# Second copies of a weight matrix made by ScalarE, VectorE and GpSimd in place of transfers, first weight passes spread over three engines, and new places for the opening's work

## The chip, the cores and the metric

The kernel runs on one core of a Trainium2 chip. The metric is the device time of one execution in microseconds: the median of 3 timed runs, 860.36 us before the change (859.08 to 860.88). Five engines work side by side, each in the order of its own instruction stream, and wait for one another through semaphores: TensorE (PE, its weight loads shown as PEld), VectorE (DVE), ScalarE (ACT), GpSimd (POOL) and SyncE (SP), which here only issues transfers. The transfers are carried by 16 DMA engines.

## The reference, cut to what matters

```python
# attention: q, k, v (8 batches, 8 heads, 576 tokens, 64 wide), tau = 0.02, float32
scores = (q @ k.T) / 8
thresh = scores.max(-1) - tau
scores = where(scores >= thresh, scores, -1e9)
attn = softmax(scores);  x = attn @ v          # heads side by side: (4608, 512)
# feed-forward: w_in (512, 1024), w_out (1024, 512), g_ln (1024)
h = x @ w_in
solu = h * softmax(h)
ln = (solu - mean(solu)) / sqrt(var(solu) + 1e-6) * g_ln
out = ln @ w_out                               # (4608, 512) float32
```

w_in and w_out arrive as 64-bit floats (a float32 array times a NumPy scalar), so that the kernel itself makes 32-bit floats of their words.

## The kernel before, in words

**Rounds.** The attention is cut into 144 slots (`slots`, L447): batch, kind (first or second 256 queries of a head pair, or the last 64 of all pairs), head pair, half. One round of the loop at L1426 handles one slot. Its phases, in order: `begin` jobs; `scores` (PE, L478); `maxes` (DVE, L500), `ramp` (ACT, L515), `exps` (ACT, L524); `early` jobs; `normalise` of the slot before (POOL, L531 to L534); `middle` jobs; matmuls of attention times v (`attend_steps`, L605, called pv below) and of the feed-forward; `blocks` of the slot before (DVE transposes, L545), and after every second slot `spread` (SP, L566 to L575), which moves the transposed weights T to wT; `late` jobs; loads. A pv comes `LAG_PV` = 3 rounds after its second slot, plus `LAG`. After it ACT copies the result (`attended`, L638).

**Opening and steady part.** Rounds 0 to 29 are the opening, rounds from START = 30 on the steady part, with other tables and PSUM tiles. In the opening the weights are decoded, the keys and queries of batches 0 and 1 are turned on PE (`turn`, L346) and kept in SBUF by ACT and DVE (`k_item`, `q_item`, `e_item`; with `EASED` the second half goes to ACT too, without it to DVE), and four tiles of 128 tokens of the feed-forward, the fronts (L1284), are run: two h steps each, a chain of jobs, two o steps, at the rounds in `HO`. `PREP` says in which round's score tile each turning is placed, `FETCH` at which round's end each load of batches 0 and 1 is issued. Up to START, `CHAIN` gives each job of a front (max, exp, mul, sum, stats, norm, norm2, turn, out, store) a phase (0 begin to 3 late) and a number of rounds after the front's second h step.

**Weights.** There are 16 pieces of 128 rows: 0 to 7 are halves of w_in, 8 to 15 are blocks of w_out. Each goes through

- `weight_load` (L261): a transfer of 512 KB to one of four raw buffers (`RAW`), which is free again after `weight_a`;
- `weight_a` (L273): three passes over the raw words: z, the high words times 2**-112 (L282 to L286, on the engine that `UNIT` names: 0 DVE, 1 ACT, 2 POOL), sg, the sign bits (L291, DVE), and the low words times 2**-29 into the destination (L294, ACT);
- `weight_b` (L306, DVE): z shifted, sg put in; `weight_c` (L316, POOL): added to the destination;
- `weight_gain` (pieces 8 to 15, L318): times g_ln, on the engine in `GAIN` (0 ACT, 1 DVE, 2 POOL);
- `weight_d` (pieces 8 to 15, L329): the second copy. PE works on 64 x 64 quarters, and `ff_o` (L1128) needs each block of w_out in both halves of the rows. So rows 0 to 63 are copied to rows 64 to 127 of the neighbouring slot of w2 and the reverse, 128 KB each, by two transfers on SP.

`PIECE` holds five places for each piece (load, a, b, c, gain and copy), counted in quarters of a round: 4 x round + phase. `weigh` (L1298) is called four times a round (before the scores, before `normalise`, after it, and at the end) and issues what is due. At a round's end everything but gain and copy stands ahead of the round's other loads, gain and copy behind them. The first o step of front 0 is in round 17, its second in round 18; the first uses pieces 8 to 11, the second 12 to 15.

**Feed-forward.** `ff_h` L1021, `ff_max`, `ff_exp` L1045, `ff_mul` L1051, `ff_sum`, `ff_stats` L1067, `ff_scale` (POOL, L1075 to L1082), `ff_norm` (ACT, L1094), `ff_norm2` (L1099: DVE, or POOL where `SECOND` says so), `ff_swap` (four transfers, L1112), `ff_turn` (DVE, L1123), `ff_o` L1141, `ff_out`, `ff_store`.

All transfers of the opening but the first few are issued by SP in program order; one that waits holds back all behind it.

Of the kernel before, what the change touches and what calls it, by code (L numbers as in the profile page):

```python
# [13 lines left out]
ALU = mybir.AluOpType  # L14
# [6 lines left out]
def kernel(  # L21
# [27 lines left out]
    nc = tc.nc  # L49
# [279 lines left out]
    def weight_d(x):  # L329
        c = x - 2 * NP  # L330
        if c >= 0:
            for r in range(2):
                nc.sync.dma_start(out=w2[ROWS[r], 2 * c + 1], in_=w2[ROWS[1 - r], 2 * c])
# [929 lines left out]
    with tc.manual_schedule():  # L1263
# [283 lines left out]
```

## Time and profile before

| | us |
|---|---|
| median of 3 runs (lowest, highest) | 860.36 (859.08, 860.88) |
| the profiled execution's own time | 858.72 |
| its span, first to last instruction | 856.9 |
| PE busy | 805.5 (94%) |
| DVE busy | 674.0 (79%) |
| ACT busy | 598.7 (70%) |
| POOL busy | 553.8 (65%) |
| start of round 0, 9, 11, 17, 19, 30 (first L500 of each) | 10.90, 53.69, 68.63, 102.96, 117.87, 172.78 |
| L333 (second copies): 16 issues, first and last | 61.8, 108.7 |
| first part of a wT spread, issue to landing, up to 130 us: least, median, greatest | 5.4, 8.0, 10.7 |

The page's line of busy tenths, 40 slices of 21.4 us, shows where PE is not full:

```profile
PE   5669789989899999999999999999999999999997
...
PEclk9879999999999999999999999999999999999999
DMA  7999886998787778877777778877788777455122
```

Each digit is the busy share of a slice in tenths, and for PEclk the clock that TensorE was granted. The chip's engines overlap, so busy times don't add up to the span. A time with a line number (L333) is that of the instructions which this line of the kernel issued.

### The profile page before, as it was taken

What the parts mean: (1) busy time and instruction counts of PE and PEld (TensorE: products, weight loads), DVE (VectorE), ACT (ScalarE), POOL (GpSimd) and SP (SyncE); (2) the same over time, 40 slices, a digit from 0 to 9 for tenths busy, and PEclk for the clock granted to TensorE, in tenths of its full rate; (3) what the DMA queues carried; (4) which work ended last, traced back from release to release, by engine and by line L of the source; (5) the groups of instructions that cost most, each with busy time, mean ns of one, the idle gap of its engine ahead of it and who ended that gap; (6) DMA issues with size and microseconds to landing.
All of it is one profiled execution on the core that took longest, in us unless ns stands there. A gap on an engine that the chain in (4) does not pass through costs nothing.

```text
span 856.9 us, 36807 instructions
## 1 busy us (share of the span) xinstructions
PE 805.5 (94%) x15345; PEld 598.5 (70%) x15345; DVE 674.0 (79%) x1335; ACT 598.7 (70%) x1205; POOL 553.8 (65%) x1020
## 2 busy tenths in 40 slices
PE   5669789989899999999999999999999999999997
PEld 3447567656577787777787787777776677777875
DVE  4978768877789788898879788888788787877451
ACT  5967967776677777777767777777877777775230
POOL 2876758865756758585857758585856757575230
PEclk9879999999999999999999999999999999999999
DMA  7999886998787778877777778877788777455122
GB/s 242 277 262 252 205 194 170 246 255 197 213 220 199 217 178 227 225 217 194 218 215 209 212 182 234 236 200 202 215 217 223 194 175 196 136 149 126 39 51 51
DMA packets 101254, 168.61 MB, mean 197 GB/s; under 512 B 18392, under 2 KB 48096, under 8 KB 101088
## 3 DMA queue, kind: packets, MB, share of 16 engines
q1 hardware_dynamic: 99952, 164.26, 72.9%
q8 instruction: 121, 1.98, 1.0%
q10 hardware_dynamic: 1136, 2.00, 0.7%
q14 instruction: 45, 0.37, 0.1%
HBM read 46.14 MB, written 9.44 MB: 65 GB/s over the span
## 4 chain that ended last, share of the span: by engine, by line
PE 68%; DMA 10%; DVE 8%; ACT 6%; SPq 3%; issue 3%; POOL 2%; DVEq 0%; ACTq 0%; POOLq 0%
PE ov L1141 17%; PE h L721 15%; PE s_ps L478 13%; PE ov L605 11%; DMA wT<-T 6%; PE o_ps L1141 5%; PE h L745 4%; DVE T L545 3%; ACT w L515 2%; DVE w L500 2%; PE h_ps L1021 2%; ACT w L524 2%; DMA V<-u 1%; DMA v<-in_v_dram 1%; PE pv L605 1%
## 5 line engine op out<-in xcount | busy, mean ns | idle before, releaser
L515 ACT ACTIVATE w<-s_ps,nth 128x576 f32<-128x576 f32 x282 | 199.6, 742 | 137.8 <-DVE nth L500 126.7
L500 DVE CUSTOM_DVE_ANT_0 w<-s_ps,tau_t 128x576 f32<-128x576 f32 x282 | 201.2, 750 | 76.8 <-PE s_ps L478 39.0
L534 POOL TENSOR_SCALAR w<-w,sm 128x576 f32<-128x576 f32 x288 | 215.6, 761 | 14.3
L524 ACT ACTIVATE w<-w,ntau 128x576 f32<-128x576 f32 x288 | 219.7, 768 | 0.0
L545 DVE STREAM_TRANSPOSE T<-w 128x576 f32<-128x576 f32 x288 | 206.4, 753 | 9.3 <-POOL w L534 7.3
L1141 PE MATMUL ov<-w,uT 64*64 64x256 f32 x3456 | 207.0, 376 | 0.0
L478 PE MATMUL s_ps<-kT,qT 64*64 64x64 f32 (+1 forms) x2048 | 179.4, 426 | 14.3 <-ACT w L515 13.3
L605 PEld LDWEIGHTS ov<-wT,v 64*64 64x64 f32 x4752 | 150.3, 133 | 51.2 <-issue 35.0
L1141 PEld LDWEIGHTS ov<-w,uT 64*64 64x64 f32 x3456 | 165.9, 133 | 20.5 <-issue 0.3
L605 PE MATMUL ov<-wT,v 64*64 64x128 f32 (+1 forms) x4752 | 153.2, 259 | 3.6 <-DMA wT<-T 3.4
L531 POOL TENSOR_SCALAR sm<-sm 128x2 f32<-128x2 f32 x144 | 37.3, 259 | 166.1 <-ACT w L524 161.8
L532 POOL TENSOR_TENSOR sm<-sm,mone 128x2 f32<-128x2 f32 x144 | 103.6, 719 | 12.0
L721 PE MATMUL h<-w,xh 64*64 64x512 f32 x832 | 104.2, 592 | 1.5 <-DVE hm L767 1.4
L478 PEld LDWEIGHTS s_ps<-kT,qT 64*64 64x64 f32 x2048 | 75.8, 140 | 37.5 <-ACT w L515 19.6
L1141 PE MATMUL o_ps<-w,uT 64*64 64x256 f32 x1152 | 70.3, 387 | 5.2 <-DVE uT L1123 2.4
L1141 PEld LDWEIGHTS o_ps<-w,uT 64*64 64x64 f32 x1152 | 56.1, 136 | 20.4 <-issue 3.6
L721 PEld LDWEIGHTS h<-w,xh 64*64 64x64 f32 x832 | 43.1, 133 | 34.6 <-issue 14.5
L1123 DVE STREAM_TRANSPOSE uT<-V 128x1024 f32<-128x1024 f32 x36 | 44.1, 1226 | 19.9 <-DMA V<-u 14.1
L524 ACT ACTIVATION_READ_ACCUMULATOR w<-w,ntau 128x1 f32 x288 | 55.8, 194 | 0.0
L721 PE MATMUL h<-k,sum 64*64 64x512 f32 x312 | 52.1, 589 | 0.0
L1099 DVE TENSOR_SCALAR u<-u,rs,nb 128x1024 f32<-128x1024 f32 x36 | 30.9, 858 | 25.9 <-ACT V L1094 25.9
L1094 ACT ACTIVATE V<-u,nb,rs 128x1024 f32<-128x1024 f32 x36 | 44.4, 1234 | 6.8 <-POOL nb L1082 5.3
(121 smaller groups left out, 999.7 us busy)
## 6 DMA issues: line engine op xcount, KB each, us to landing
wT<-T SPq DMA_DIRECT2D x132, 288.0 KB, 4.6
wT<-T SPq DMA_DIRECT2D x256, 144.0 KB, 3.9
V<-u SPq DMA_DIRECT2D x144, 64.0 KB, 2.2
out_dram<-ob SPq DMA_DIRECT2D x71, 128.0 KB, 2.8
wT<-T SPq DMA_DIRECT2D x14, 576.0 KB, 7.2
q<-in_q_dram SPq DMA_DIRECT2D x24, 288.0 KB, 5.1
qT<-flip SPq DMA_DIRECT2D x48, 144.0 KB, 3.7
q<-in_k_dram SPq DMA_DIRECT2D x24, 288.0 KB, 5.0
```

Of the source, the lines that this page charges most:

```text
L478: nc.tensor.matmul(out=ps[h][ROWS[y], ks], lhsT=lhsT, rhs=d["kT"][ROWS[h], ks], start=True, stop=True,)
L500: nc.vector.tensor_tensor_reduce(out=w, in0=ps[:, 0:S], in1=(zero if loose else tau_t).to_broadcast([P, S]), scale=1.0, scalar=BIG, op0=AL ...
L515: nc.scalar.activation(out=d["w"][x], in_=d["w"][x] if d["loose"] else d["ps"][x][:, 0:S], func=AF.Prelu, bias=d["nth"][x], scale=-1.0, al ...
L524: nc.scalar.activation(out=w, in_=w, func=AF.Exp, bias=ntau, scale=1.0, accum_out=sm[:, x : x + 1])
L532: nc.gpsimd.tensor_tensor(out=sm, in0=sm, in1=mone, op=ALU.pow)
L534: nc.gpsimd.tensor_scalar(out=w, in0=w, scalar1=sm[:, x : x + 1], scalar2=1.0, op0=ALU.mult, op1=ALU.mult)
L545: nc.vector.transpose(out=T[:, :, r, :, h, :], in_=w.rearrange("p (c m x) -> p c m x", c=2, x=32))
L605: nc.tensor.matmul(out=to, lhsT=d["v"][ROWS[u], (h0 + h - u) % 4 if b > 1 else h0 + h, m ^ 4 * u if m < 8 and b < 2 else m,], rhs=rhs, sta ...
L721: mm = nc.tensor.matmul(out=h[ROWS[y], 512 * bank : 512 * bank + 512], lhsT=x[ROWS[r], ROWS[y]], rhs=w[ROWS[r]], start=c == 0 and (n, r, k ...
L1094: nc.scalar.activation(out=V, in_=u, func=AF.Identity, bias=nb, scale=rs)
L1123: nc.vector.transpose(out=uT, in_=d["V"].rearrange("p y (m x) -> p m y x", x=32))
L1141: nc.tensor.matmul(out=d["o"][ROWS[z], of : of + 256], lhsT=d["uT"][ROWS[r], m].rearrange("p y x -> p (y x)"), rhs=w2[ROWS[r], m ^ r, 256 ...
```

## The change

- `weight_d` asks a new table, `MOVER`, for each half copy (index 2 x piece + half): 0 an ACT copy, 1 a DVE and 2 a POOL multiplication by 1, 3 the transfer as before. Of the 16 half copies 5 are on ACT, 3 on POOL, 1 on DVE, 7 stay transfers.
- Gain and copy become two jobs. The copy has a place of its own, `MOVE`, or else that of the gain.
- `UNIT`: the first pass z, all on DVE before, is on POOL for pieces 1, 2, 3 and 5, on ACT for 4, 6, 7, 8 and 10 to 13, and on DVE for 0, 9, 14 and 15.
- `GAIN`: all on ACT before; now DVE for 8 and 10, POOL for 12 and 15.
- `PIECE`, `EASED`, `SECOND`, `PREP`, `LAG`, `FETCH`, `HO`, `CHAIN` have other numbers: weight loads 8 and 10 to 13 and 15 are later by two to four quarters, load 7 earlier by two, among others; fronts 1 and 3 have `norm2` on POOL. The change in `HO` (30 to 32) has no effect, as everything from 30 on goes to the steady part. Of `EASED`, only rounds that turn something count: 14 (to 0), 19 and 20 (to 1).

```diff
--- before.py
+++ after.py
@@ -327,10 +327,24 @@
 
 
     def weight_d(x):
+
         c = x - 2 * NP
         if c >= 0:
             for r in range(2):
-                nc.sync.dma_start(out=w2[ROWS[r], 2 * c + 1], in_=w2[ROWS[1 - r], 2 * c])
+                to, of = w2[ROWS[r], 2 * c + 1], w2[ROWS[1 - r], 2 * c]
+                by = MOVER[2 * x + r]
+                if by == 0:
+                    nc.scalar.copy(out=to, in_=of)
+                elif by == 1:
+                    nc.vector.tensor_scalar(
+                        out=to, in0=of, scalar1=1.0, scalar2=None, op0=ALU.mult
+                    )
+                elif by == 2:
+                    nc.gpsimd.tensor_scalar(
+                        out=to, in0=of, scalar1=1.0, scalar2=1.0, op0=ALU.mult, op1=ALU.mult
+                    )
+                else:
+                    nc.sync.dma_start(out=to, in_=of)
 
 
 
@@ -928,18 +942,20 @@
     }
     SPLIT = {30: 0, 32: 8, 34: 1, 36: 1, 38: 20, 40: 30, 42: 17, 44: 27, 46: 20, 56: 27, 74: 21, 92: 23, 110: 26, 128: 14}
     SEVEN = {0: 21, 1: 21, 2: 24, 3: 25, 4: 25, 5: 26, 7: 26, 6: 29}
-    PIECE = {0: (-1, 1, 3, 6, 7), 1: (-1, 3, 7, 10, 11), 2: (-1, 7, 11, 14, 15), 3: (3, 11, 15, 18, 19), 4: (3, 15, 19, 22, 23), 5: (7, 19, 23, 26, 27), 6: (11, 23, 27, 30, 31), 7: (15, 27, 31, 34, 35), 8: (19, 31, 35, 38, 39), 9: (23, 35, 39, 42, 43), 10: (27, 39, 43, 46, 47), 11: (31, 43, 47, 50, 51), 12: (35, 47, 51, 54, 55), 13: (39, 51, 55, 58, 59), 14: (43, 55, 59, 62, 63), 15: (51, 59, 63, 66, 67)}
+    PIECE = {0: (-1, 1, 3, 6, 7, ), 1: (-1, 3, 5, 10, 11, ), 2: (-1, 8, 11, 14, 15, ), 3: (3, 12, 15, 18, 19, ), 4: (3, 15, 18, 21, 25, ), 5: (7, 20, 23, 26, 27, ), 6: (11, 23, 25, 30, 31, ), 7: (13, 27, 31, 34, 35, ), 8: (23, 31, 35, 38, 39, ), 9: (23, 35, 39, 42, 43, ), 10: (29, 39, 43, 46, 47, ), 11: (35, 43, 47, 50, 51, ), 12: (39, 49, 51, 54, 55, ), 13: (43, 52, 55, 58, 59, ), 14: (43, 55, 59, 62, 63, ), 15: (55, 59, 63, 66, 67, )}
     RAW = {0: 0, 1: 1, 2: 2, 3: 3, 4: 0, 5: 1, 6: 2, 7: 3, 8: 0, 9: 1, 10: 2, 11: 3, 12: 0, 13: 1, 14: 2, 15: 0}
     QUEUE = {0: 1, 1: 1, 2: 1, 3: 0, 4: 0, 5: 0, 6: 0, 7: 0, 8: 0, 9: 0, 10: 0, 11: 0, 12: 0, 13: 0, 14: 0, 15: 0}
-    UNIT = {0: 0, 1: 0, 2: 0, 3: 0, 4: 0, 5: 0, 6: 0, 7: 0, 8: 0, 9: 0, 10: 0, 11: 0, 12: 0, 13: 0, 14: 0, 15: 0}
-    GAIN = {8: 0, 9: 0, 10: 0, 11: 0, 12: 0, 13: 0, 14: 0, 15: 0}
-    EASED = {0: 1, 1: 1, 2: 1, 3: 1, 4: 1, 5: 1, 6: 1, 7: 1, 8: 1, 9: 1, 10: 1, 11: 1, 12: 1, 13: 1, 14: 1, 15: 1, 16: 1, 17: 0, 18: 0, 19: 0, 20: 0, 21: 0}
-    SECOND = {0: 0, 1: 0, 2: 0, 3: 0}
-    PREP = {0: 14, 1: 14, 2: 14, 3: 15, 4: 15, 5: 16, 6: 16, 7: 16, 8: 19, 9: 19, 10: 19, 11: 20, 12: 20, 13: 21, 14: 21, 15: 21}
-    LAG = {1: 1, 3: 1, 5: 1, 11: 1, 17: 1}
-    FETCH = {0: 10, 1: 10, 2: 11, 3: 11, 4: 15, 5: 15, 6: 16, 7: 16, 8: 17, 9: 18, 10: 24, 11: 25, 12: 0, 13: 1, 14: 3, 15: 5}
-    HO = {0: 11, 1: 12, 2: 17, 3: 18, 4: 13, 5: 14, 6: 22, 7: 23, 8: 20, 9: 21, 10: 26, 11: 27, 12: 24, 13: 25, 14: 30, 15: 30}
-    CHAIN = {0: (3, 0), 1: (3, 0), 2: (3, 1), 3: (3, 1), 4: (2, 2), 5: (0, 3), 6: (2, 3), 7: (3, 4), 8: (0, 1), 9: (3, 1), 10: (3, 2), 11: (3, 2), 12: (3, 3), 13: (3, 3), 14: (2, 4), 15: (0, 5), 16: (2, 5), 17: (3, 6), 18: (0, 1), 19: (3, 1), 20: (3, 0), 21: (3, 0), 22: (3, 1), 23: (3, 1), 24: (2, 2), 25: (0, 3), 26: (2, 3), 27: (3, 4), 28: (0, 1), 29: (3, 1), 30: (3, 0), 31: (3, 0), 32: (3, 1), 33: (3, 1), 34: (2, 2), 35: (0, 3), 36: (2, 3), 37: (2, 6), 38: (0, 1), 39: (3, 1)}
+    UNIT = {0: 0, 1: 2, 2: 2, 3: 2, 4: 1, 5: 2, 6: 1, 7: 1, 8: 1, 9: 0, 10: 1, 11: 1, 12: 1, 13: 1, 14: 0, 15: 0}
+    GAIN = {8: 1, 9: 0, 10: 1, 11: 0, 12: 2, 13: 0, 14: 0, 15: 2}
+    MOVER = {16: 0, 17: 0, 18: 2, 19: 1, 20: 2, 21: 0, 22: 3, 23: 3, 24: 0, 25: 0, 26: 3, 27: 3, 28: 3, 29: 2, 30: 3, 31: 3}
+    MOVE = {8: 47, 9: 55, 10: 55, 13: 63, 14: 70, 15: 67}
+    EASED = {0: 0, 1: 1, 2: 1, 3: 1, 4: 1, 5: 1, 6: 1, 7: 0, 8: 1, 9: 1, 10: 0, 11: 1, 12: 0, 13: 0, 14: 0, 15: 1, 16: 1, 17: 0, 18: 0, 19: 1, 20: 1, 21: 0}
+    SECOND = {0: 0, 1: 1, 2: 0, 3: 1}
+    PREP = {0: 14, 1: 14, 2: 14, 3: 15, 4: 15, 5: 17, 6: 16, 7: 16, 8: 19, 9: 19, 10: 18, 11: 20, 12: 20, 13: 22, 14: 21, 15: 21}
+    LAG = {1: 2, 3: 1, 5: 1, 9: 1, 11: 1, 17: 0, 21: 0, 25: 0}
+    FETCH = {0: 10, 1: 8, 2: 8, 3: 11, 4: 15, 5: 15, 6: 13, 7: 16, 8: 17, 9: 21, 10: 24, 11: 25, 12: 0, 13: 0, 14: 3, 15: 5}
+    HO = {0: 11, 1: 12, 2: 17, 3: 18, 4: 13, 5: 14, 6: 22, 7: 23, 8: 20, 9: 21, 10: 26, 11: 27, 12: 24, 13: 25, 14: 32, 15: 32}
+    CHAIN = {0: (3, 0), 1: (3, 0), 2: (3, 1), 3: (1, 2), 4: (2, 2), 5: (0, 3), 6: (2, 3), 7: (3, 4), 8: (0, 1), 9: (3, 1), 10: (3, 2), 11: (3, 2), 12: (3, 3), 13: (3, 3), 14: (2, 4), 15: (0, 5), 16: (1, 6), 17: (3, 6), 18: (0, 1), 19: (0, 1), 20: (3, 0), 21: (0, 1), 22: (0, 2), 23: (3, 1), 24: (2, 2), 25: (3, 2), 26: (2, 3), 27: (3, 4), 28: (2, 1), 29: (3, 1), 30: (3, 0), 31: (3, 0), 32: (3, 1), 33: (1, 2), 34: (2, 2), 35: (2, 2), 36: (1, 4), 37: (1, 6), 38: (0, 1), 39: (2, 2)}
 
     CHAINED = "max", "exp", "mul", "sum", "stats", "norm", "norm2", "turn"
 
@@ -1286,16 +1302,19 @@
         SECOND.update({t: SECOND.get(x) for x, t in enumerate(fronts)})
         weights = {}
         for x in range(NW):
-            def rest(x):
-                weight_gain(x)
+            def copies(x):
                 weight_d(x)
                 made.add(x)
 
-            jobs_of = zip((2, 3, 1, 0, 4), (weight_load, weight_a, weight_b, weight_c, rest), PIECE[x])
+            jobs_of = zip(
+                (2, 3, 1, 0, 4, 5),
+                (weight_load, weight_a, weight_b, weight_c, weight_gain, copies),
+                (*PIECE[x], MOVE.get(x, PIECE[x][4])),
+            )
             for n, job, when in jobs_of:
                 weights.setdefault(when, []).append((n, x, job))
 
-        def weigh(phase, ns=range(5)):
+        def weigh(phase, ns=range(6)):
             for n, x, job in sorted(weights.get(4 * rnd + phase, []), key=lambda j: j[:2]):
                 if n in ns:
                     job(x)
@@ -1509,7 +1528,7 @@
             weigh(3, range(4))
             for job in load_at.pop(rnd, []):
                 job()
-            weigh(3, (4,))
+            weigh(3, (4, 5))
             rnd += 1
 
 
```

## The prediction

> **What bounds the kernel now.** I read first the page's busy shares by slice, then the same shares over stretches cut at the rounds. A round begins at its first L500: round 0 at 10.90 us, 9 at 53.69, 11 at 68.63, 17 at 102.96, 19 at 117.87, 30 (START) at 172.78. Columns: busy time and instructions of each engine, granted TensorE clock, DMA share, GB/s.
>
> ```profile
> 10.90:53.70 42.80, 29.87 (x529) 18.17 (x522) 38.62 (x83) 37.40 (x86) 31.84 (x42) 0.85 0.99 262
> 53.70:68.60 14.90, 11.69 (x179) 8.88 (x183) 8.16 (x19) 8.96 (x18) 9.91 (x14) 0.62 1.00 273
> 68.60:103.00 34.40, 29.44 (x586) 20.72 (x578) 29.45 (x58) 29.20 (x67) 24.24 (x35) 1.00 0.93 229
> 103.00:117.90 14.90, 12.40 (x234) 8.80 (x238) 8.72 (x21) 10.11 (x21) 9.63 (x19) 0.89 0.92 214
> 117.90:172.80 54.90, 52.53 (x1148) 37.78 (x1140) 47.18 (x94) 40.26 (x83) 40.90 (x67) 1.00 0.82 201
> 172.80:240.00 67.20, 60.94 (x1127) 39.64 (x1125) 52.30 (x101) 45.78 (x94) 44.96 (x85) 1.00 0.85 213
> 240.00:600.00 360.00, 356.68 (x6856) 274.14 (x6852) 308.32 (x616) 269.29 (x537) 248.94 (x473) 1.00 0.79 212
> ```
>
> From 240 to 600 us PE works 99% of the time; nothing in the change touches that, so its result is what it does to the arrival at START. In rounds 0 to 8 (42.8 us, 4.76 a round) DVE is busy 90% and the DMA engines 99%. Rounds 9 and 10 take 7.45 us each with the transfers at 1.00 and the clock at 0.62. From 68.6 to 117.9 PE loses 4.96 and 2.50 us to gaps.
>
> Then the chain of waits and the waits by pair (total us, times, longest), which name the gaps:
>
> ```profile
> 53.44 10.45 DMA wT<-T
> 108.72 4.40 DMA w<-w
> ...
> DVE w L500 <- ACT w L322: 5.8, 2, 3.0
> PEld o_ps L1141 <- DMA w<-w: 2.7, 1, 2.7
> PE o_ps L1141 <- DMA w<-w: 2.2, 1, 2.2
> PE pv L605 <- DMA wT<-T: 1.8, 3, 1.1
> ```
>
> The first is the spread of round 8, whose transposed weights come 10.45 us after issue, behind weight loads, so that PE stands in round 10's pv. The second is the last copy of w_out (L333): front 0's second o half stops 2.2 us for it. The 5.8 us of DVE are those same PE stalls passed on: ACT reaches L322 only after the attended copy (L638) that waits for pv.
>
> Last the queue of SP and the rows that price the moved work:
>
> ```profile
> 97.55 1.99 SPq L132 DMA_DIRECT2D k<-in_k_dram  x2
> 99.63 1.15 SPq L333 DMA_DIRECT2D w<-w  x2
> 100.88 0.60 SPq L566 DMA_DIRECT2D wT<-T  x1
> 101.53 3.74 SPq L568 DMA_DIRECT2D wT<-T  x2
> 105.32 1.98 SPq L132 DMA_DIRECT2D q<-in_q_dram  x2
> 107.40 1.91 SPq L333 DMA_DIRECT2D w<-w  x2
> ...
> 55.52 1.28 POOL L316 TENSOR_TENSOR w<-w,em 128x512 int32<-128x512 int32 x1
> 64.55 0.65 DVE L306 SCALAR_TENSOR_TENSOR em<-em 128x512 int32<-128x512 int32 x1
> 52.02 1.06 DVE L306 SCALAR_TENSOR_TENSOR em<-em 128x512 int32<-128x512 int32 x1
> ```
>
> From 88.9 to 109.9 us SP issues almost without a pause, so what is taken out of its queue brings the rest forward.
>
> **The change, part by part.** Prices: DVE's L286 starts its successor 0.34 us later (12.27 to 12.60). POOL has no such pass; its L534 takes 1.47 us for two of 576 columns, so 0.65 for 512; the other end is 1.28, the two-input L316. I take 0.66, since L534 too has one input. ACT reads the same raw words in L294, 0.57 us from start to start (60.48 to 61.05); I take that for a first pass, and 0.6 for a gain or a copy (L322, mean 726 ns, 0.6 to its successor). No row shows an engine copying from one half of the rows to the other. It has the free size of these, 512, on half the rows; between half the price (0.3) and double (1.3) I take 0.6 on ACT, 0.66 on POOL, 0.34 on DVE. A copy issue costs SP 0.6 to 0.95 us (1.15 to 1.91 for two) and moves 128 KB, 0.5 us of transfers at 245 GB/s.
>
> *Rounds 0 to 8.* First passes of pieces 1, 2, 3, 5 go to POOL, of 4, 6, 7, 8 to ACT: DVE loses 8 x 0.34 = 2.7 us, POOL gains 4 x 0.66 = 2.6, ACT 4 x 0.57 = 2.3. DVE was the fullest, so at best -2.7. But POOL runs 3.9 us of a 4.7 us round (sum 0.24, pow 0.71, two L534 1.47, L316 1.28 and gaps); three of its passes fall in rounds 2, 3 and 5, ahead of a normalise, and what is late next is L545, which queues all of DVE behind it: at worst +2.0. And a round that ends sooner only reaches the late transfers sooner. I take -1.0.
>
> *Rounds 9 and 10.* Piece 11 is loaded one round later, behind the spread of round 8 instead of ahead: 0.5 MB, 1.9 us at 273 GB/s. Piece 8's two copies leave the queue (-1.0 us of transfers for what follows). Against it, two key/query loads come forward to round 8, but behind that spread in SP's order; pieces 8 and 9 are still both ahead of round 6's spread, so round 9's wait stays. Bounds: -5.4 (both rounds back to 4.76) and +1.0. I take -1.5.
>
> *Rounds 11 to 16.* Nine of sixteen copies leave the transfers in all: 1.2 MB, 4.7 us of DMA time and some 7 us of SP. ACT gains 4 passes (2.3) and 5 copies (3.0), loses 4 gains (2.4): 29.2 becomes 32.1 of 34.4. POOL gains 2 gains and 2 of its 3 copies: 2.6. DVE is even (four passes less, two gains, a copy and some keeps of round 14 more). PE's 4.96 us of gaps are partly issue pauses of 2.0 us at 90.9 and partly waits for ACT. Bounds -3.0 and +2.5; I take -1.0, as the transfers were at 0.93 but POOL had no pause from 83.1 to 95.6.
>
> *Rounds 17 and 18.* Piece 15's gain moves from ACT (104.17, behind the attended copy and an exponential) to POOL, free at 101.0. Its copies stay transfers; ahead of them one query load of 1.0 us is gone from round 16. A half copy of piece 14 is issued behind them in round 17 and is needed 12 matmuls earlier. So not all of 2.2 goes: -1.2, between -2.6 and 0.
>
> *Rounds 19 on.* Two L1099 (0.85 each) leave DVE for POOL, 1024/576 x 0.735 = 1.3 each. The first comes into POOL's 7.1 us wait before 122.65 and is hidden by it, the second into 1.8 us before 169.46. If that cover were gone, normalise and L545 would be 1.3 late each time. The swaps behind them issue 4 transfers each as before. Chain places, score preparation and the one pv that moves a round earlier (LAG 17) shift within PE's 2.4 us of gaps: -0.3, between -1.0 and +1.5. After START nothing.
>
> Sum: -1.0 - 1.5 - 1.0 - 1.2 - 0.3 = -5.0. The profiled span 856.9 becomes 851.9, its run of 858.72 becomes 853.7. That run lies 1.64 below the median shown, 860.36, from which I subtract the same: 855.4.
>
> **Two rules against the rows.** The Trainium skill, page "SBUF — State Buffer", section "SBUF: two separate sides", says that GpSimd and a DVE instruction in a two-port mode or with two SBUF inputs exclude each other for the whole instruction. The trace agrees in kind: L306 takes 0.65 alone and 1.06 beside L316. By the rule the passes given to POOL are paid on DVE too; that is the second rival below.
>
> The clock was granted at 0.62 in rounds 9 and 10, where PE had 3.2 us of gaps. The skill's page "TensorE: Matmul & The Clock Gate", section "Part 1: The HAM clock gate", says that idle time throttles the clock and activity frees it. By that rule, fewer gaps would give more than their own length; that is the first rival.
>
> **Rivals.**
> *1. The gaps close and the clock comes with them.* Rounds 9 and 10 held 11.69 us of PE work at 0.62; at full clock 0.62 x 11.69 = 7.2, 4.4 us less. If the wait for wT goes, -4.5 takes the place of -1.5, and with -2.0 instead of -1.0 in rounds 11 to 16 the sum is -9.0: 851.4. For it: two rounds of 7.45 against 4.76. Against it: transfers of 1.00 from 20 us on, with only 0.5 MB taken from ahead.
>
> *2. POOL becomes the bound: slower.* At the end of round 13 it gets three instructions at once (gain of piece 12, copies of 9 and 10), 2.0 us, in the stretch with no pause, ahead of front 0's statistics (L1075 to L1082); for their last ACT's L1094 waited already at 91.3, and round 15's L515 is queued behind it. With the three passes of rounds 2, 3 and 5 that is 4.0 us late, and each of nine added POOL instructions may hold L306 for 1.06 - 0.65 = 0.4 us, 3.6 more. It decides once POOL's work in a round passes its length, 4.7 us: 3.9 + 0.66 + 0.4 does. Full price +7.6, less the -1.2 and -1.5 of the transfers and half of DVE's 2.7: about +3.5, 863.9. Against it: POOL waits 0.3 to 1 us in most early rounds for ACT's L524.
>
> *3. The transfers were hidden anyway.* The wT of round 6 and the piece loads stay ahead as they are, the transfer engines remain full, rounds 9 and 10 keep their length, and the saved DVE time turns into waiting for them; only the 1.2 of round 18 is left, less 0.5 elsewhere: 859.7. The change then moves the work and hardly the time.
>
> **Chances.** Forecast 0.42 (853 to 858.6), rival 1 0.20, rival 3 0.15, rival 2 0.23. What a measurement of this kernel can tell from no change is 0.2%, 1.7 us: the forecast and rival 1 are faster, 0.62; rival 3 is the same, 0.15; rival 2 slower, 0.23. The range runs from 849.5, below rival 1, to 863.5, into rival 2, leaving out under 2 in 10. The forecast's own range is 852 to 859.
>
> **What would show it.** L333 with 7 issues instead of 16; L286 with 4 on DVE. Right: rounds 9 and 10 together at 13.4 us or less, the wait of o_ps for w<-w under 1.2 us, START reached near 168. Rival 1: clock above 0.8 between rounds 9 and 11. Rival 2: L545 waiting for POOL's L534 in rounds 2 to 5 by over 0.5 us more, and L1094 waiting longer for nb. Rival 3: START within 1.5 us of 172.8 and the waits for wT as long. I would be wrong altogether if the span changed after 240 us, or if a load of piece 15, issued a round later but used at the same place, stopped DVE at the end of round 14.

## The result and the profile after

The changed kernel takes 855.59 us (median of 20 runs, 847.98 to 861.80) where the kernel before, run beside it, takes 860.19 (median of 20, 852.80 to 863.94): a ratio of 0.9943 (95% interval 0.9915 to 0.9971). Measured a second time it was 855.22 against 858.40, again 0.9943 (0.9910 to 0.9976). Ratios here and below are taken over the runs in the fast state alone, so they differ somewhat from the quotients of the medians beside them. The profiled execution took 855.74 us with a span of 853.3 (before: 858.72 and 856.9). The lines of the page that stood at L500, L515, L524, L534, L545, L605 and L1141 are now L514, L529, L538, L548, L559, L619 and L1157; the copies are L347 (transfer), L337 (ACT), L343 (POOL) and L339 (DVE).

The stages of the changed kernel, cut at the first L514 of rounds 0, 9, 11, 17, 19, 30 and 35, with the columns of the windows before (busy time and instructions of PE, PEld, DVE, ACT, POOL; granted clock; DMA share; GB/s):

```profile
10.38:54.26 43.88, 30.01 (x533) 18.93 (x525) 37.37 (x75) 39.45 (x90) 35.25 (x46) 0.89 0.97 270
54.26:65.32 11.06, 8.14 (x178) 6.68 (x180) 8.31 (x18) 8.14 (x17) 8.79 (x13) 0.84 1.04 263
65.32:100.24 34.92, 29.93 (x586) 20.43 (x578) 30.63 (x60) 32.62 (x70) 27.79 (x41) 1.00 0.84 218
100.24:112.53 12.29, 10.40 (x228) 6.96 (x232) 8.46 (x19) 9.39 (x22) 9.76 (x20) 1.00 0.84 193
112.53:171.97 59.44, 54.43 (x1156) 43.10 (x1152) 45.72 (x89) 41.64 (x89) 45.63 (x75) 0.97 0.85 210
171.97:200.18 28.21, 25.43 (x403) 16.86 (x399) 20.59 (x39) 16.48 (x34) 14.10 (x25) 0.94 0.92 235
```

The reader is to see that rounds 0 to 8 are no shorter (43.88 against 42.79), rounds 9 and 10 lose 3.9 us and get clock back (0.62 to 0.84), rounds 17 and 18 lose 2.6, and rounds 19 to 29 gain length again (59.44 against 54.91). START comes at 171.97 against 172.78, and round 35 at 200.18 against 200.52: in this one pair of profiles hardly anything is left by round 35.

A pair of profiles misleads here, because executions of one kernel differ by several us. So both kernels were profiled a second time: the changed one as `again`, the one before as `twin`. Their lines for rounds 9 and 10, first `again`:

```profile
54.64:67.09 12.45, 9.91 (x180) 7.59 (x184) 8.06 (x18) 7.89 (x17) 7.69 (x11) 0.68 0.98 240
```

and `twin`, with rounds 17 and 18 as its second line:

```profile
54.03:71.43 17.40, 11.33 (x180) 9.30 (x184) 9.75 (x19) 8.37 (x19) 10.88 (x15) 0.64 0.96 255
106.52:120.69 14.17, 11.93 (x220) 8.27 (x224) 8.73 (x21) 9.99 (x20) 9.40 (x18) 0.90 0.95 217
```

Here rounds 9 and 10 took 12.45 and 17.40. All stages, from the first L500 or L514 of one round to that of the next, in us:

| rounds | before, twin | after, again | difference of the means | predicted |
|---|---|---|---|---|
| 0 to 8 | 42.79, 42.98 | 43.88, 43.79 | +0.9 | -1.0 |
| 9 and 10 | 14.94, 17.40 | 11.06, 12.45 | -4.4 | -1.5 |
| 11 to 16 | 34.33, 35.09 | 34.92, 34.25 | -0.1 | -1.0 |
| 17 and 18 | 14.91, 14.17 | 12.29, 12.56 | -2.1 | -1.2 |
| 19 to 29 | 54.91, 59.22 | 59.44, 59.36 | +2.3 | -0.3 |
| 30 to 34 | 27.74, 27.24 | 28.21, 27.12 | +0.2 | 0 |
| 0 to 34 | 189.62, 196.10 | 189.80, 189.53 | -3.2 | -5.0 |

By round 35 the profiles give -3.2, and the two of the kernel before alone lie 6.5 apart; the medians of the timed runs give -4.6 and -3.2. From round 47 to 143 the four profiles agree within 0.7 us (512.49, 512.41, 512.24, 511.86): nothing is gained there, as predicted. (In all fourteen profiles, those of the experiments included, this stretch takes 509.9 to 512.7 us, so even there two profiles can differ by 2 to 3 us.) The end behind round 143 differs too (80.13 and 77.86 before, 78.36 and 77.82 after), and in the first pair makes up 1.8 of the span's 3.6.

The two waits that named the gaps are still there. From the chain of waits of the changed kernel (start, us, what was waited for), and then from its waits by pair between 54.26 and 112.53 us (total, times, longest):

```profile
54.01 8.27 DMA wT<-T
```

```profile
PE pv L619 <- DMA wT<-T: 2.9, 3, 1.8
...
PE o_ps L1157 <- DMA w<-w: 1.8, 1, 1.8
```

The spread of round 8 now lands 8.27 us after its issue instead of 10.45 (12.77 in `twin`). PE's waits for wT in rounds 9 and 10 by this view are 2.9 us here against 1.8, and 1.0 in `again` against 2.7 in `twin`, but the view misses one. In front of round 9's first pv the kernel before has a gap that the profile puts under "issue":

```profile
55.08 0.69 PE L605 MATMUL pv<-wT,v 64*64 64x128 f32 x4 [2.02 <-issue]
```

The second part of round 6's spread was issued at 43.82 us and landed 11.17 us later, at 54.99: this gap too ends with a landing of wT. The same holds in `twin` (a gap of 3.97, landing at 57.33, pv at 57.42) and in `again` (1.60, 55.99, 56.08). In the changed kernel's first profile that part lands at 53.53 and there is no such gap. So the waits for wT are 3.9 and 6.7 us before and 2.9 and 2.6 after: they did shrink, most of all in front of round 9. The stop of the second o half is 1.8 us instead of 2.2 (2.07 in `again`, 2.24 in `twin`) and shrank by little.

### The profile page after: what moved, and what is told of

The parts are those of the page before. It is cut to its first block, busy times and chain, and to the rows that moved or that the text cites. A ratio compares the mean times of both kernels' runs of the same rounds, so it can differ in the third digit from the quotient of the medians.

```text
span 853.3 us, 36829 instructions
## 1 busy us (share of the span) xinstructions
PE 800.5 (94%) x15345; PEld 600.4 (70%) x15345; DVE 672.0 (79%) x1324; ACT 603.3 (71%) x1214; POOL 561.5 (66%) x1031
## 4 chain that ended last, share of the span: by engine, by line
PE 68%; DMA 10%; ACT 6%; DVE 5%; POOL 4%; issue 3%; SPq 2%; DVEq 0%; ACTq 0%; POOLq 0%
PE ov L1157 17%; PE h L735 15%; PE s_ps L492 12%; PE ov L619 11%; DMA wT<-T 7%; PE o_ps L1157 5%; PE h L759 4%; ACT w L529 2%; DVE T L559 2%; ACT w L538 2%; PE h_ps L1037 2%; PE pv L619 2%; DVE w L514 1%; DMA V<-u 1%; POOL w L548 1%
## 5 line engine op out<-in xcount | busy, mean ns | idle before, releaser
L529 ACT ACTIVATE w<-s_ps,nth 128x576 f32<-128x576 f32 x282 | 199.4, 741 | 136.7 <-DVE nth L514 123.9
L514 DVE CUSTOM_DVE_ANT_0 w<-s_ps,tau_t 128x576 f32<-128x576 f32 x282 | 201.1, 749 | 79.3 <-PE s_ps L492 49.5
L548 POOL TENSOR_SCALAR w<-w,sm 128x576 f32<-128x576 f32 x288 | 216.0, 762 | 14.3
L538 ACT ACTIVATE w<-w,ntau 128x576 f32<-128x576 f32 x288 | 219.7, 768 | 0.0
L559 DVE STREAM_TRANSPOSE T<-w 128x576 f32<-128x576 f32 x288 | 206.3, 752 | 9.8 <-POOL w L548 8.7
L1157 PE MATMUL ov<-w,uT 64*64 64x256 f32 x3456 | 206.2, 376 | 0.0
L492 PE MATMUL s_ps<-kT,qT 64*64 64x512 f32 (+1 forms) x2048 | 174.1, 421 | 17.2 <-ACT w L529 16.3
L619 PEld LDWEIGHTS ov<-wT,v 64*64 64x64 f32 x4752 | 149.1, 133 | 52.3 <-issue 35.8
L1157 PEld LDWEIGHTS ov<-w,uT 64*64 64x64 f32 x3456 | 167.4, 133 | 18.1
L619 PE MATMUL ov<-wT,v 64*64 64x128 f32 (+1 forms) x4752 | 151.5, 258 | 4.5 <-DMA wT<-T 3.9
L545 POOL TENSOR_SCALAR sm<-sm 128x2 f32<-128x2 f32 x144 | 35.0, 243 | 145.6 <-ACT w L538 141.3
L492 PEld LDWEIGHTS s_ps<-kT,qT 64*64 64x64 f32 x2048 | 72.7, 137 | 41.8 <-ACT w L529 23.3
L1157 PE MATMUL o_ps<-w,uT 64*64 64x256 f32 x1152 | 66.6, 377 | 4.5 <-DVE uT L1139 2.2
L1157 PEld LDWEIGHTS o_ps<-w,uT 64*64 64x64 f32 x1152 | 57.9, 133 | 14.8 <-issue 3.8
L538 ACT ACTIVATION_READ_ACCUMULATOR w<-w,ntau 128x1 f32 x288 | 55.8, 194 | 0.0
L1115 DVE TENSOR_SCALAR u<-u,rs,nb 128x1024 f32<-128x1024 f32 x34 | 29.2, 860 | 26.1 <-ACT V L1110 26.1
```

Source lines behind the costliest of these rows:

```text
L492: nc.tensor.matmul(out=ps[h][ROWS[y], ks], lhsT=lhsT, rhs=d["kT"][ROWS[h], ks], start=True, stop=True,)
L514: nc.vector.tensor_tensor_reduce(out=w, in0=ps[:, 0:S], in1=(zero if loose else tau_t).to_broadcast([P, S]), scale=1.0, scalar=BIG, op0=AL ...
L529: nc.scalar.activation(out=d["w"][x], in_=d["w"][x] if d["loose"] else d["ps"][x][:, 0:S], func=AF.Prelu, bias=d["nth"][x], scale=-1.0, al ...
L538: nc.scalar.activation(out=w, in_=w, func=AF.Exp, bias=ntau, scale=1.0, accum_out=sm[:, x : x + 1])
L548: nc.gpsimd.tensor_scalar(out=w, in0=w, scalar1=sm[:, x : x + 1], scalar2=1.0, op0=ALU.mult, op1=ALU.mult)
L559: nc.vector.transpose(out=T[:, :, r, :, h, :], in_=w.rearrange("p (c m x) -> p c m x", c=2, x=32))
```

## The experiments

Twelve kernels were run in three groups of four, in the order of the table. Each group shared a chip and its runs of the kernel before (medians 858.23, 858.40 and 857.83). All ratios are to those.

| kernel | median us | ratio, 95% interval |
|---|---|---|
| copies_alone | 860.85 | 1.0051, 1.0014 to 1.0088 |
| transfers | 857.60 | 1.0002, 0.9973 to 1.0031 |
| passes_back | 857.19 | 0.9992, 0.9963 to 1.0020 |
| loads_back | 858.11 | 1.0005, 0.9974 to 1.0037 |
| again (the changed kernel) | 855.22 | 0.9943, 0.9910 to 0.9976 |
| out_early | 854.21 | 0.9949, 0.9920 to 0.9977 |
| three | 854.19 | 0.9926, 0.9893 to 0.9959 |
| places_back | 857.63 | 0.9996, 0.9961 to 1.0031 |
| late_copies | 854.64 | 0.9958, 0.9931 to 0.9986 |
| values_early | 854.07 | 0.9969, 0.9937 to 1.0001 |
| both | 853.97 | 0.9952, 0.9923 to 0.9981 |
| twin (the kernel before) | 859.48 | 1.0000, 0.9967 to 1.0033 |

### Which part is the gain: four parts apart

**copies_alone** is the kernel before with the new `weight_d`, `MOVER`, `MOVE` and the split of gain and copy; every other table is the old one.

```diff
+    MOVER = {16: 0, 17: 0, 18: 2, 19: 1, 20: 2, 21: 0, 22: 3, 23: 3, 24: 0, 25: 0, 26: 3, 27: 3, 28: 3, 29: 2, 30: 3, 31: 3}
+    MOVE = {8: 47, 9: 55, 10: 55, 13: 63, 14: 70, 15: 67}
```

> The kernel before with the nine half copies on ACT, POOL and DVE at the changed kernel's places, all other tables as before. Theory (transfers were what cost): the copies are the heart of the change; with 1.2 MB less to move round 11 stays near 68.6 us (no copy was ahead of round 8's spread), rounds 11 to 18 gain 2 to 4 us, and the time falls by 2 to 4 us against before (856 to 858). Rival (the order of the loads and the other places make the gain, the copies were hidden): within 1.5 us of before.

It was measured slower, 860.85 (1.0051), where both expectations had it faster or level: rounds 9 and 10 took 19.01, rounds 11 to 16 36.40, 17 and 18 15.47. The nine copies taken off the transfers are worth nothing by themselves. Part of the price is seen in round 15: PE waits 2.07 us for a key that ACT keeps (L420) behind the norm of front 0. In the two profiles of the kernel before, with the same places but with transfers for copies, PE's waits for a kept key in rounds 11 to 16 are 0.3 us at most.

**transfers** is the changed kernel with all copies as transfers, in the new places.

```diff
-    MOVER = {16: 0, 17: 0, 18: 2, 19: 1, 20: 2, 21: 0, 22: 3, 23: 3, 24: 0, 25: 0, 26: 3, 27: 3, 28: 3, 29: 2, 30: 3, 31: 3}
+    MOVER = {16: 3, 17: 3, 18: 3, 19: 3, 20: 3, 21: 3, 22: 3, 23: 3, 24: 3, 25: 3, 26: 3, 27: 3, 28: 3, 29: 3, 30: 3, 31: 3}
```

> The changed kernel with all sixteen half copies as transfers again, at the changed places. Theory: it gives back 2 to 3 of the 4.6 us; SP issues sixteen copies, the second o half of front 0 waits longer for w than 1.8 us, round 19 begins later than 114 us (112.5 in the changed kernel's profile). Rival: round 19 begins within 1 us of 112.5 and the time is within 1.5 us of the changed kernel's.

It is back at the time of before, 857.60. Its rounds 9 and 10 were the shortest of all (10.62), so the copies are not needed for that; its rounds 17 and 18 took 16.06, the longest of all. The timeline shows why, SP's queue first, then PE (start, us, engine, line, what, count, and in brackets the idle time before):

```profile
103.10 2.88 SPq L347 DMA_DIRECT2D w<-w  x4
...
110.54 3.25 PE L1157 MATMUL o_ps<-w,uT 64*64 64x256 f32 x26 [3.61 <-DMA w<-w]
```

Four copies stand behind one query load, and the second o half stops 3.61 us for the last of them; its next 26 matmuls then take 3.25 us.

**passes_back** has the first passes and gains on the engines of before.

```diff
-    UNIT = {0: 0, 1: 2, 2: 2, 3: 2, 4: 1, 5: 2, 6: 1, 7: 1, 8: 1, 9: 0, 10: 1, 11: 1, 12: 1, 13: 1, 14: 0, 15: 0}
-    GAIN = {8: 1, 9: 0, 10: 1, 11: 0, 12: 2, 13: 0, 14: 0, 15: 2}
+    UNIT = {0: 0, 1: 0, 2: 0, 3: 0, 4: 0, 5: 0, 6: 0, 7: 0, 8: 0, 9: 0, 10: 0, 11: 0, 12: 0, 13: 0, 14: 0, 15: 0}
+    GAIN = {8: 0, 9: 0, 10: 0, 11: 0, 12: 0, 13: 0, 14: 0, 15: 0}
```

> The changed kernel with all first passes on DVE and all gains on ACT, as before. Theory of POOL as the bound in round 5: in the changed kernel DVE waited 2.4 us for POOL's normalise behind the pass of piece 5, and round 9 began 0.6 us later than before though DVE had 2.7 us less to do; without the passes round 6 begins near 39.5 us (40.9 there) and the time is the same or up to 1.5 us better than the changed kernel's. Rival (DVE's relief is worth its 2.7 us): round 9 begins 1.5 to 2.5 us later than 54.3, the time is 1.5 to 3 us worse than the changed kernel's.

857.19, two us above the changed kernel, with intervals that overlap. The time came out as the rival said and the stage as neither said: round 5 took 4.46 us instead of 6.70, but rounds 0 to 4 took 25.49 instead of 23.84, and rounds 0 to 8 43.92 against 43.88 and 43.79. Taking eight passes off DVE does nothing for the stage in which DVE was fullest.

**loads_back** has the loads of the pieces (the first number of each entry of `PIECE`) as before, everything else new. Here and below only the numbers that differ are shown.

```diff
-PIECE[7][0], [8], [10], [11], [12], [13], [15] = 13, 23, 29, 35, 39, 43, 55
+PIECE[7][0], [8], [10], [11], [12], [13], [15] = 15, 19, 27, 31, 35, 39, 51
```

> The changed kernel with the weight loads at the places of before (the first number of each piece), all else changed. Theory: rounds 9 and 10 gained 3.9 us because piece 11's load no longer stands ahead of round 8's spread; with it back there, the spread lands later by some 2 us and rounds 9 and 10 take 13 to 15 us instead of 11.1, the time rises by 2 to 3 us against the changed kernel. Rival (they gained since the two copies of piece 8 and the DVE passes went): the two rounds stay within 1 us of 11.1.

858.11, all of the gain gone. Rounds 9 and 10 took 13.82 at a clock of 0.64. That one reading lies inside the spread of the kernels with the new loads (10.6 to 14.0 in nine profiles, 16.2 in one, mean 12.6), so the stage alone decides nothing; the timed runs say that the later loads matter. Taken together, the four profiles with the old loads (13.8, 14.9, 17.4 and 19.0, mean 16.3) lie above all but two of the ten with the new ones. But the way in which the loads should act is not seen: round 8's spread landed 8.72 us after its issue here, hardly later than the 8.27 of the changed kernel, and what the two rounds take beyond its 11.06 us is lost clock (10.45 us of PE at 0.64).

**places_back** has `EASED`, `SECOND`, `PREP`, `LAG`, `FETCH`, `HO` and `CHAIN` as before and keeps the rest of the change.

> The changed kernel with the tables of turning, lag, loads of keys, queries and values, and fronts' chains as before; only copies, passes, gains and the weights' places are new. Theory: what the new places lose in rounds 20 and 29 comes back (round 20 near 5.5 us, round 29 near 4.4), and the wait of o_ps for w grows again in part, as the query load of pair 6 stands ahead of the last copies; in sum 0 to 3 us better than the changed kernel. Rival (the places found anew are what carries the gain): the time is that of before or slower.

857.63, again the time of before. What the theory said of single rounds came: round 20 took 5.54 us (9.22 in the changed kernel), round 29 4.42 (7.87), and rounds 9 and 10 were the second shortest of all (10.86). But rounds 11 to 16 took 36.90, with a wait of PE for ACT's kept key of 1.83 us as in copies_alone, and rounds 17 and 18 15.71:

```profile
104.88 1.83 SPq L132 DMA_DIRECT2D q<-in_q_dram  x2
106.81 2.10 SPq L347 DMA_DIRECT2D w<-w  x3
...
113.87 1.54 PE L1157 MATMUL o_ps<-w,uT 64*64 64x256 f32 x24 [3.35 <-DMA w<-w]
```

Two query loads instead of one are ahead of the three copies, since `FETCH` of load 6 is at round 16 again, and the stop is 3.35 us. The same lines of the changed kernel:

```profile
101.73 1.14 SPq L132 DMA_DIRECT2D q<-in_q_dram  x1
102.97 2.97 SPq L347 DMA_DIRECT2D w<-w  x3
...
109.06 1.53 PE L1157 MATMUL o_ps<-w,uT 64*64 64x256 f32 x24 [1.79 <-DMA w<-w]
```

One query load, three copies, 1.79 us. Three copies behind two query loads stop PE for 3.35 us (2.90 in copies_alone), four behind one for 3.61: for this stop each of the two edits is worth nothing without the other. All three kernels are worse than the one before (2.23); they also have the new, later place of a half copy of piece 14, which stands in the same queue, and no run separates that.

**again** is the changed kernel.

> The changed kernel unaltered, to be read beside the others on one chip. Theory: about 0.994 of before. In its profile round 5 lasts 6.7 us, rounds 17 and 18 together 12.3, round 29 some 7 to 8, as in its first profile; rounds 9 and 10 vary, since wT's landing did in all profiles so far. Rival (the gain was one chip's): within 0.2% of before.

855.22, the same ratio as the first time. Its stages are in the table above; round 5 took 6.76 us and round 29 7.61, as expected.

### What the changed kernel still loses

**out_early** moves one job: the o result of front 2 is written out two phases earlier.

```diff
-CHAIN[28] = (2, 1)
+CHAIN[28] = (0, 1)
```

> The changed kernel with front 2's result copied out at the beginning of a round as before (entry 28 of CHAIN (0, 1), not (2, 1)). Theory: in round 29 PE stands 2.8 us in front of pv, whose PSUM tile ACT frees only behind the exponentials of the round; with the copy first, round 29 lasts 4.4 to 5 us instead of 7 to 8, START comes 2 to 3 us earlier and the time falls by 2 to 3 us against the changed kernel. Rival (the next wait takes its place: wT of round 28's spread lands at 167, and transfers are at 0.9 to 1.0 until 200): round 31 begins less than 1 us earlier.

854.21 (0.9949): no difference from the changed kernel that can be told. In the changed kernel round 29, which took 4.42 and 6.46 us before, takes 7.87 and 7.61, and the timeline blames ACT's o copy:

```profile
166.18 0.54 PE L619 MATMUL pv<-wT,v 64*64 64x128 f32 x4 [2.80 <-ACT ob L1176]
```

In out_early that copy is early, and the same matmuls wait for their transposed weights instead:

```profile
168.04 0.64 PE L619 MATMUL pv<-wT,v 64*64 64x128 f32 x4 [1.41 <-DMA wT<-T]
```

With the wait of the 66 matmuls behind them (0.65 and 0.78 us, for wT in both kernels), 3.45 us of waiting became 2.19, and round 29 became 6.43. The transfers were the next to be late, and the time did not follow.

**three** is out_early with two more reversals: the first pass of piece 5 on DVE, and no second halves of keys on ACT in rounds 19 and 20.

```diff
-CHAIN[28], UNIT[5], EASED[19], EASED[20] = (2, 1), 2, 1, 1
+CHAIN[28], UNIT[5], EASED[19], EASED[20] = (0, 1), 0, 0, 0
```

> The changed kernel with three steps undone: front 2's copy out as in out_early, the first pass of piece 5 on DVE (round 5 took 6.7 us with it on POOL, 4.3 before), and the second halves of the turned keys and queries of rounds 19 and 20 on DVE again (round 20 took 7.6 to 9.2 us, 5.5 before). Theory: round 5 under 5.2 us, round 20 under 7, round 29 under 5.5; 4 to 6 us better than the changed kernel. Rival (the opening waits for transfers, which swallow all but round 29's share): 2 to 3 us better, as out_early.

854.19 (0.9926; the medians alone give 0.9951): the 4 to 6 us did not come. Of the three marks one was met. Round 5 fell from 6.70 to 4.45, and rounds 0 to 4 rose from 23.84 to 25.29, as in passes_back. Round 20 fell to 7.57, not under 7, and rounds 19 to 21 fell from 17.34 to 15.74; transfers, which keeps these keys on ACT, has the same 7.57 and 15.69, so the fall can't be put down to the edit. Round 29 took 7.36 although out_early's edit is in it. Rounds 17 and 18 rose from 12.29 to 14.19: behind a stop of 2.05 us the last 24 matmuls of the o step took 2.32 us instead of 1.53, and the granted clock of the two rounds was 0.88 instead of 1.00.

**late_copies** makes the last three transferred halves of the copies that stop front 0 on DVE and POOL.

```diff
-MOVER[28], MOVER[30], MOVER[31] = 3, 3, 3
+MOVER[28], MOVER[30], MOVER[31] = 1, 2, 1
```

> The changed kernel with its last three transferred half copies that round 18 waits for on engines too: the first half of piece 14 on DVE, the halves of piece 15 on POOL and DVE. Theory (rounds 17 and 18 wait for the last copy in SP's queue; five profiles have 12.1 to 12.6 us with one query load and three copies there, 14.9 to 16.1 with more): the wait of o_ps for w goes, rounds 17 and 18 take 10.5 to 11 us, and the time falls by 1 to 2 us against the changed kernel (to 853.5 to 854.5). Rival (what is gained before round 28 is taken back where the transfers are full, from 160 to 200 us): the rounds are as short, but rounds 29 to 34 grow by as much and the time is within 0.7 us of the changed kernel's.

854.64 (0.9958). The wait of the o matmuls for w<-w is gone, all 64 of the second step run in 3.63 us, and yet rounds 17 and 18 take 12.08 instead of 12.29 and 12.56. The timeline, ACT and then DVE:

```profile
112.55 1.24 ACT L1110 ACTIVATE V<-u,nb,rs 128x1024 f32<-128x1024 f32 x1 [1.16 <-POOL nb L1098]
...
114.63 0.76 DVE L514 CUSTOM_DVE_ANT_0 w<-s_ps,zero 128x576 f32<-128x576 f32 x1 [2.88 <-ACT kT L420]
```

Round 19's first instruction on DVE stands 2.88 us for ACT's kept keys, which stand behind the next front's norm, itself 1.16 us late from POOL. In the changed kernel the same instruction waits for the same keys:

```profile
112.53 0.76 DVE L514 CUSTOM_DVE_ANT_0 w<-s_ps,zero 128x576 f32<-128x576 f32 x1 [3.07 <-ACT kT L420]
```

There PE ends the o step, stop included, at 110.59, while ACT, its norm 1.16 us late as here, reaches the copy of the o result at 111.40 and the keys at 112.06 without another wait. So in this profile the norm's chain, and not the stop for the copies, already set the start of round 19; in `again` PE ended 0.38 us later than that chain. The edit took away a wait that hardly ended last any more. Neither the 10.5 to 11 us of the theory nor the longer rounds 29 to 34 of the rival (34.76; 36.08 and 34.73 in the changed kernel) came.

**values_early** fetches three late value loads two to three rounds earlier, so that they do not stand ahead of round 28's spread, with out_early's edit.

```diff
-FETCH[9], FETCH[10], FETCH[11], CHAIN[28] = 21, 24, 25, (2, 1)
+FETCH[9], FETCH[10], FETCH[11], CHAIN[28] = 19, 21, 22, (0, 1)
```

> The changed kernel with front 2's copy out at the round's beginning and three value loads of batch 1 issued two to three rounds earlier (round 21's at 19, 24's at 21, 25's at 22), into the stretch from 115 to 150 us where the transfer engines are at 0.55 to 0.8. Theory (START is bound by transfers: in seven profiles with the new places rounds 29 to 34 take 32.7 to 36.1 us, with wT late in round 29 and in round 34): 0.75 MB less before 160 us, wT waits under 1 us in round 29, rounds 29 to 34 take 31.5 to 33 us, 1 to 2 us better than out_early. Rival (the loads from round 28 on, for batch 2, fill the engines whatever goes before): rounds 29 to 34 stay at 33.5 to 35 us.

854.07 (0.9969). The wait for wT in round 29 is gone, the round takes 4.97, and rounds 29 to 34 take 33.03 (36.08 and 34.73 in the changed kernel). But then

```profile
173.52 2.54 PE L759 MATMUL h<-w,xh 64*64 64x512 f32 x16 [2.29 <-POOL w L692]
```

the steady part's first h step stands 2.29 us for POOL, and rounds 9 and 10 happened to take 13.99. The time is that of the changed kernel.

**both** is late_copies and values_early together.

> late_copies and values_early together. Theory: the gains add, 2 to 4 us under the changed kernel, 851 to 853, and this is the fastest version so far. Rival: as the parts of the change, they don't add; between 853 and 855.

853.97 (0.9952). Both edits hold (rounds 17 and 18 at 12.09, round 29 at 4.97), and rounds 9 and 10 took 16.20 in its profile, which neither edit touches. No version can be told from the changed kernel: the five have medians of 853.97 to 854.64 and intervals that overlap its own.

**twin** is the kernel before.

> The kernel before, unaltered, as a control and for a second profile. The ratio must be 1 within 0.3%. Theory (rounds 9 and 10 are long in the kernel before as such): they take 13 to 19 us, against 10.6 to 13.1 in the profiles with the new load places. Rival (one late landing in one profile): 11 to 12.5 us.

859.48 (1.0000 of the same kernel's other runs). Rounds 9 and 10 took 17.40, as the theory said. Its profile reached round 35 at 207.15 us, 6.6 later than the first profile of the same kernel; most of the difference is in rounds 9 and 10 (2.5) and 22 to 29 (4.2).

## Why the prediction was right, point by point

The time was forecast at 855.4 and came to 855.59, and the sum of -5.0 stands against a measured -4.6 and -3.2. The direction and the size were right; that the figure was met within 0.2 us was luck. The measured interval is 2.4 us wide to either side, and the terms of the sum were not right: two were too small, one too large, and the gains of rounds 0 to 8 and of 19 to 29 were not there. They miss the means of the profiles by 0.9 to 2.9 us each, some up and some down, and so nearly cancel.

**Rounds 0 to 8: -1.0 predicted, none gained.** The stage took 43.9 and 43.8 us against 42.8 and 43.0; copies_alone, whose rounds 0 to 8 have the old passes and places, took 43.9, so I read no gain, and a loss of up to 1 us. The step that failed is that DVE's relief is worth a third of its size. DVE lost eight L286, 2.7 us from start to start, and its busy time fell by 1.25 (0.7 between `twin` and `again`). A POOL pass cost not 0.66 but 0.85 to 0.97 us (0.70 to 0.99 in `again`). Where a POOL instruction ran beside it, L291 often took 0.76 to 0.92 instead of 0.41, and the ten L291 rose from 4.1 us to 4.9 (5.8 in `again`). And DVE's waits for POOL's normalise rose from 1.3 and 2.0 us to 3.2 and 3.8, most of it in one place:

```profile
33.87 0.94 POOL L286 TENSOR_SCALAR em<-raw 128x512 f32<-128x512 f32 x1
...
38.02 1.51 DVE L559 STREAM_TRANSPOSE T<-w 128x576 f32<-128x576 f32 x2 [2.38 <-POOL w L548]
```

The pass of piece 5 runs ahead of L316 and the normalise of round 5, and DVE stands 2.38 us where it stood at most 0.4 before (0.9 in `twin`). That is the second rival's mechanism, at the place it named and over its mark of 0.5 us; its price was at most 1 us in the stage, of the 7.6 it was given in all. Its sign at `nb` did not show: the norm's waits for it from round 9 to 18 are 1.8 and 1.7 us against 1.5 and 2.1 before. At 19.03 us a POOL L286 of 0.97 us began beside a L291 of 0.39; in `again` a L291 of 0.79 began at 18.79, beside a POOL L316 that ran until 19.28, and the L286 behind that took 0.70. The Trainium skill's rule that GpSimd and certain DVE instructions exclude each other ("SBUF — State Buffer", "SBUF: two separate sides") agrees in kind with these pairs; no row shows whether L291, which has one input, is of that kind.

**Rounds 9 and 10: -1.5 predicted, about -4.4 measured.** The mechanism was to be the later loads. The time of loads_back bears out that they matter; how they act stays open, since the spread of round 8 landed there almost as early as in the changed kernel. The size was the first rival's (-4.5), but about half of it (2.3 us) lies in round 9, whose wait the prediction let stay: it is for round 6's spread, and it varies from one profile to the next, from 0 (loads_back) to 4.3 us in the four profiles with the old loads and from 0.4 to 4.0 in the ten with the new. That half is not shown to come from the change. PE's busy time at the granted clock splits the stage: 11.69 us at 0.62 is 7.2 us of work and 4.4 of lost clock, with 3.2 of gaps beside it. Over the two profiles of each kernel the means are

| rounds 9 and 10, us | before, twin | after, again |
|---|---|---|
| work at full clock | 7.2, 7.3 | 6.8, 6.7 |
| lost to the clock | 4.4, 4.1 | 1.3, 3.2 |
| gaps of PE | 3.2, 6.1 | 2.9, 2.5 |

so 2.0 of the 4.4 us are clock and 1.9 gaps; 0.5 of busy time is left that the clock does not account for. The first rival's sign, a clock above 0.8, appeared in one profile of two, and its condition, that the wait for wT goes, in none: 2.9 and 2.6 us of it are left (3.9 and 6.7 before, with the gap in front of round 9, which the prediction's view of the waits has under "issue"). So a part of the clock comes back with a part of the gaps. That is the way in which the Trainium skill says that idle time throttles the clock ("TensorE: Matmul & The Clock Gate", "Part 1: The HAM clock gate"); no run here shows how long a gap may be.

**Rounds 11 to 16: -1.0 predicted, nothing found.** The transfers were indeed relieved (share 0.93 to 0.84), but they did not bound the stage. PE's gaps were 4.96 us before and 4.99 after; ACT's busy time rose from 29.2 to 32.6 and POOL's from 24.2 to 27.8 (32.1 and 26.8 were worked out), and PE's waits for the exponentials (L515, now L529) rose from 1.8 to 2.5 us, while its pauses of issue shrank from 2.3 to 1.6. The cost of a copy was well sized: ACT 0.63, POOL 0.61, DVE 0.42 against 0.6, 0.66 and 0.34. What the sum left out is that the copies and the places hang together: with the copies and the old tables of places the stage took 36.40 and 36.90 us (copies_alone, places_back), the longest of all fourteen profiles (the others 33.9 to 35.6), so here the new places earn back what the copies cost.

**Rounds 17 and 18: -1.2 predicted, -2.1 measured.** The step was that the stop for w<-w falls by 1.2; it fell by 0.2 to 0.4, and to 1.2 it did not come, so the mark set for it was missed. What went instead: 1.3 us of lost clock (12.40 and 11.93 us busy at 0.89 and 0.90, now 10.40 at 1.00), 0.5 of PE's busy time besides, and only 0.4 of gaps. transfers, places_back and copies_alone show that the wait does depend on both edits named in the prediction, the one query load fewer and the copies, and that neither has a share of its own. late_copies shows that had the wait gone altogether, hardly more would have come (12.08 us).

**Rounds 19 to 29: -0.3 predicted, +2.3 found between the means (+0.1 to +4.5).** Three moves add up to it. Rounds 19 to 21 lose 1.8 us (15.29 and 15.42 to 17.34 and 17.06); this goes with the new places (15.3 to 15.4 us in the four profiles with the old ones, 15.7 to 17.5 in the ten with the new), but which of the tables sets it is not shown: three has 15.74 with the keys of rounds 19 and 20 off ACT, and transfers 15.69 with them on it. Rounds 22 to 28 gain 1.8 (35.20 and 37.34 to 34.23 and 34.69). Round 29 loses 2.3 us (4.42 and 6.46 to 7.87 and 7.61), first to the o copy that CHAIN put late and behind it to the transfers; places_back, with the old places, has 4.42. `EASED` had no price in the sum and the places of `CHAIN` were put under "PE's 2.4 us of gaps", with +1.5 as the upper bound; and the transfers, at 0.92 to 1.02 in rounds 29 to 34, give back what comes early. There the third rival was right in its mechanism.

**START near 168 predicted, 171.97 and 173.26 found.** Both meet the third rival's sign instead, within 1.5 us of 172.8. The two marks were set from one profile of before (172.78), and its twin came at 179.91: either sign read alone would have said the wrong thing about the time.

**What bounded the kernel.** The prediction read each gap as a term that an edit removes. The experiments show several terms close to each other: where one edit took a wait away (out_early, late_copies, values_early), another of transfers, ACT, POOL or clock ended last within 1 to 3 us. I take that to be why the four parts, undone one at a time, each bring the time back to 857.2 to 858.1, 2 to 3 us of a gain of 3 to 5, and why the copies alone make it 0.5% slower; no run shows it for the whole. passes_back, whose interval overlaps the changed kernel's most, is the least sure of the four. The shares cannot be given singly: the differences between these four are smaller than their intervals.

## What to carry to other kernels

Where several engines and the transfers are all nearly full, price an edit by what ends second there, not by the wait that it removes, and expect parts of a joint change to be worth nothing or less when taken alone. Take a second profile of the kernel before as soon as stages of a few us are to be compared, since here one execution differed from the next by more than the whole change. Where the granted clock is low in a stage, write its PE time as work, lost clock and gaps: gaps that shrink a little can go with more clock than their own length (in rounds 17 and 18 here 0.4 us of gaps and 1.3 of clock). Where a view of waits says "issue" in front of an instruction that needs transferred data, compare its start with the landing of the transfer before pricing the waits.

## What the runs showed of the hardware

- Executions of one kernel on one core scatter by several us: 847.98 to 861.80 for the changed one, 850.51 to 862.57 for twin; the two profiles of the kernel before differ by 6.5 us in the first 35 rounds, by 0.1 from round 47 to 143, and by 2.3 behind it.
- After waits of PE of about 2 us, the matmuls behind them sometimes run at a lower pace and sometimes not: in the first profile of before ten took 1.54 us behind a stop of 2.23, in twin ten took 0.87 behind a stop of 2.24; 24 took 2.32 in three behind 2.05, and 1.53 in the changed kernel behind 1.79. In before the clock granted in the 3.4 us behind that stop was 0.54, in the changed kernel 1.00.
- A copy of 64 x 512 floats from one half of the rows to the other takes ACT 0.63 us, POOL 0.61 and DVE 0.42 (0.78 and 0.79 in late_copies and both, beside a POOL instruction), as much as a pass over all 128 rows (ACT's first pass 0.57 from start to start, DVE's L286 0.42).
- POOL's first pass over raw words takes 0.70 to 0.99 us (the estimate was 0.66); a gain of the same size (L324) takes POOL 0.69 and DVE 0.48.
